# DeltaNet attention and a cosine router: a 32-column inverse, a block-diagonal state and a computed order of steps

## The chip, the cores and the metric

The kernel runs on one core of one Trainium2 chip. A core has five engines, each with its own in-order queue of instructions: TensorE (PE in the profile, PEld for its weight loads), VectorE (DVE), ScalarE (ACT), GpSimd (POOL) and SyncE (SP), which here issues DMAs. [...] Matrix products land in PSUM, eight banks of 2 KB in each of 128 partitions, and VectorE or ScalarE must move them to SBUF, the working memory. The metric is the device time of one execution in microseconds (us). Beside it stands the span, the time from the first to the last instruction in one profiled execution.

## The reference

```python
def _attn_ref(q, k, v, beta):                    # (4, 8, 768, 48) each, beta (4, 8, 768)
    k_n = k / (np.linalg.norm(k, axis=-1, keepdims=True) + 1e-06)
    for t in range(S):
        y[:, :, t] = np.einsum('bhd,bhde->bhe', q[:, :, t], state)
        v_old = np.einsum('bhde,bhd->bhe', state, kt)
        state = state + bt[:, :, :, None] * np.einsum('bhd,bhe->bhde', kt, vt - v_old)
    ...
def _moe_ref(x, expert_emb, tau, w1, w2):        # x (3072, 384), 8 experts, hidden 1024
    logits = xn @ en.T / tau
    expert_idx = np.argmax(logits, axis=1)
    ...
        h = np.maximum(x[mask] @ w1[e], 0.0)
        out[mask] = gate_w[mask, None] * (h @ w2[e])
```

The first half is a linear attention whose 48x48 state for each batch and head is corrected by every token (the delta rule), so tokens depend on each other in order. The second half sends each of the 3,072 tokens to the one of 8 experts whose embedding has the largest cosine with it, and scales the result by the gate. All is in float32.

## The kernel before

The attention works through 12 chunks of 64 tokens (`C`). Of four batches two make a unit: 24 units in all, unit n being chunk n // 2 and batch pair n % 2. Token t of batch i lies in partition 64 i + t, and 8 heads lie along the free dimension. Within a chunk the recurrence becomes linear algebra: a triangular 64x64 matrix for each head and batch, made of products of keys (`gram`, lines 363 to 379), must be inverted, and its inverse applied to the values less what the old state predicts.

The inverse grows by doubling. `W` holds the inverse of the diagonal blocks of 2, and each pair of steps, `level` (line 412) and `grow` (line 417) for s in 2, 4, 8, 16, doubles the block to 32; the last doubling is done on the values by `solve1`, `solve2` and `solve3`. `level` multiplies the gram matrix with the transposed inverse `T`, and VectorE writes the part below the diagonal that the masks `below[s]` name into a prepared identity, `P`; `grow` multiplies `P` with `W`. Both use `product` (line 403): 16 matmuls of 64x64 by 64, of which successive ones take the four quarters of TensorE's array, from partition half a to half b. As the product moves data from one half to the other, an operand is kept in two layouts, and `flip` (line 381) transposes whole 128x128 pairs of heads on TensorE: one for the gram matrix (`a_flip`), three for the inverse (`t_flip`) in every unit. `apply` (line 448) is the other form: one matmul for each head and batch, 16 in all, that stays within its half, so it takes two quarters of the array. The solves and `outputs` use it.

The state lies as `S_u[u]`, a 48x48 block per head and batch in partitions 0 to 47 or 64 to 111; `of_state` (line 425) multiplies it with transposed keys or queries, 16 matmuls of 48x64 by 48. After the outputs come `x_transposes`, `logits` and the routing steps `route1` to `route6`, every second chunk for its four units, and `put_on_lists`, which writes token numbers to per-expert lists in DRAM by indirect DMAs on POOL.

PSUM is shared out as two single banks (`bank`, line 87) and three double ones (`pair`, line 90).

The order of all instructions within their queues is written out by hand: `PLAN` gives each step of a unit a time, units follow each other every `PERIOD` = 20 of those times, and steps are issued in the order of n * PERIOD + time. A step issues its matmuls and its evictions together, so neighbouring dependent steps of a unit stand about 3 times apart and those of three to five units are interleaved between them. `first_weights` loads the first expert's weights on SP in 14 pieces from unit 5 on.

When all lists are written, the expert stage gathers tokens in tiles of 128 by expert and runs both expert layers (`work_through`, line 785): 28 tiles were worked on in the profiled run.

## Time and profile before

| | us |
|---|---|
| median of three timed runs | 800.41 (799.04 to 801.53) |
| profiled execution, own time | 800.33 |
| its span | 798.6 |
| first gram (L325, pair<-KT) | 14.43 |
| first level (pair<-T,AJ) | 28.39 |
| gram of unit 3, gram of unit 23 | 61.8, 406.4 |
| first expert matmul (L723) | 479.7 |
| TensorE busy from 100 to 380 us | 36 to 38 in each 40 |
| POOL pow (L340), each | 1.65 |
| copy_predicated 128x512 (L415), each | 0.73 |
| ScalarE copy, 128x512 and 128x384 | 0.60, 0.49 |

The attention takes the first 480 us and the expert stage the rest. In the profile a line such as `pair<-W,P` names the tile written and those read; L325 is the helper that issues nearly all matmuls, so the groups must be told apart by their tiles: pair<-T,AJ and pair<-T,G are levels, pair<-W,P grows, bank<-ident,W and bank<-ident,G flips, bank<-R,W the first and third solve, bank<-Z,G the second solve and the outputs, pair<-S,KT the state products, pair<-Z,KK the state update, pair<-KT gram. Each float32 matmul makes two records, so 16 matmuls are 32 records; a transposition makes one. Busy times of matmuls overlap, as they are pipelined: what a step takes is read from the start of one step to the start of the next. "issue" as a releaser means that the engine waited for nothing that the profile shows.

### The profile page before, as it was taken

How to read it: one execution, taken by the hardware profiler on the slowest of the kernel's cores; microseconds unless marked ns; L12 is line 12 of the kernel's file. 1: busy time of each engine (PE TensorE's matmuls, PEld its weight loads, DVE VectorE, ACT ScalarE, POOL GpSimd, SP SyncE). 2: the span in 40 equal slices, each digit the busy share in tenths (PEclk: the TensorE clock that was granted, in tenths of full speed). 3: DMA queues.
4: the chain of work that ended last, by engine and by line, in shares of the span. 5: the costliest groups of instructions: out<-in, count | busy, mean ns of one | idle time of the engine just before them, and what ended most of it. 6: DMA issues, size and time to landing. Idle time of an engine off the chain costs nothing.

```text
span 798.6 us, 32885 instructions
## 1 busy us (share of the span) xinstructions
PE 705.7 (88%) x15002; PEld 603.9 (76%) x15002; DVE 281.7 (35%) x644; ACT 240.6 (30%) x463; POOL 223.9 (28%) x257
## 2 busy tenths in 40 slices
PE   2578899998999998999988729999999999999993
PEld 2567888887888887888877628877888877788872
DVE  5465455554555555555544231011011011011010
ACT  3344454454445444445433201001111010111010
POOL 4542333423444342345121121111111111111110
PEclk9699999999999999999999658999999999999997
DMA  6336422321142131111001029999999999999996
GB/s 114 62 109 159 121 39 49 69 41 34 34 86 53 35 77 34 24 25 46 5 5 45 20 49 375 391 367 336 329 316 334 330 313 335 338 319 332 311 323 236
DMA packets 135342, 132.20 MB, mean 166 GB/s; under 512 B 84154, under 2 KB 119393, under 8 KB 135202
## 3 DMA queue, kind: packets, MB, share of 16 engines
q1 hardware_dynamic: 130450, 118.76, 48.3%
q0 software_dynamic: 4544, 11.27, 3.7%
q8 instruction: 119, 1.95, 1.0%
q14 instruction: 21, 0.17, 0.1%
q10 hardware_dynamic: 208, 0.05, 0.0%
HBM read 118.39 MB, written 12.45 MB: 164 GB/s over the span
## 4 chain that ended last, share of the span: by engine, by line
PE 58%; DMA 17%; issue 12%; DVE 6%; ACT 5%; SPq 0%; POOL 0%; POOLq 0%; ACTq 0%; DVEq 0%
PE pair L325 19%; DMA out_dram<-y,ids 16%; PE bank L325 15%; PE acc L723 8%; PE acc L730 7%; PE bank L385 6%; ACT G L373 2%; PE bank L360 1%; PE bank L501 1%; ACT W L401 1%; DVE P L415 1%; DVE W L376 1%; ACT KT L401 1%; DVE XC L492 1%; PE acc L714 1%
## 5 line engine op out<-in xcount | busy, mean ns | idle before, releaser
L725 ACT ACTIVATE hT<-acc 128x512 f32<-128x512 f32 x56 | 33.5, 598 | 279.9 <-PE acc L723 264.7
L723 PEld LDWEIGHTS acc<-xTm,w 128*128 128x128 f32 x864 | 99.3, 192 | 4.8
L723 PE MATMUL acc<-xTm,w 128*128 128x128 f32 x864 | 99.4, 275 | 0.0
L730 PE MATMUL acc<-w,hT 128*128 128x384 f32 x288 | 95.9, 486 | 0.0
L733 POOL DMA_INDIRECT out_dram<-y,ids x28 | 28.5, 1017 | 228.6 <-DVE y L732 211.5
L415 DVE COPY_PREDICATED P<-below,pair 128x512 f32<-128x512 int32 x96 | 70.1, 732 | 51.7 <-PE pair L325 42.4
L325 PE MATMUL pair<-W,P 64*64 64x64 f32 x3072 | 75.6, 224 | 13.3 <-issue 8.3
L401 ACT ACTIVATE W<-pair 128x512 f32<-128x512 f32 x96 | 57.5, 599 | 92.0 <-PE pair L325 86.6
L340 POOL TENSOR_TENSOR rn<-rn,half 128x8 f32<-128x8 f32 x24 | 39.5, 1646 | 139.9 <-DVE rn L339 105.6
L730 PEld LDWEIGHTS acc<-w,hT 128*128 128x128 f32 x288 | 53.3, 190 | 33.4
L325 PEld LDWEIGHTS pair<-W,P 64*64 64x64 f32 x3072 | 64.5, 136 | 17.5 <-issue 10.7
L715 DVE COPY xTm<-acc 128x384 f32<-128x384 f32 x29 | 16.2, 558 | 151.9 <-PE acc L714 151.9
L325 PE MATMUL bank<-Z,G 64*64 64x48 f32 x1536 | 59.6, 225 | 7.9 <-issue 7.5
L325 PE MATMUL bank<-R,W 64*64 64x48 f32 x1536 | 59.3, 223 | 8.1 <-issue 5.5
L732 DVE TENSOR_SCALAR y<-acc,xg 128x384 f32<-128x384 f32 x28 | 17.3, 618 | 129.0 <-PE acc L730 129.0
L325 PEld LDWEIGHTS bank<-R,W 64*64 64x64 f32 x1536 | 53.9, 140 | 10.6 <-issue 10.0
L325 PEld LDWEIGHTS bank<-Z,G 64*64 64x64 f32 x1536 | 53.6, 140 | 9.7 <-issue 8.4
L723 PEld LDWEIGHTS acc<-xTm,w_first 128*128 128x128 f32 x480 | 57.2, 198 | 3.5 <-DVE xTm L715 1.1
L723 PE MATMUL acc<-xTm,w_first 128*128 128x128 f32 x480 | 57.4, 281 | 0.7 <-DVE xTm L715 0.7
L730 PE MATMUL acc<-w_first,hT 128*128 128x384 f32 x160 | 53.3, 486 | 0.0
L325 PE MATMUL pair<-T,AJ 64*64 64x64 f32 x1536 | 40.5, 228 | 11.1 <-DVE T L393 7.0
L385 PE MATMUL bank<-ident,W 128*128 128x128 f32 x288 | 47.9, 289 | 1.3 <-ACT W L401 1.1
(167 smaller groups left out, 987.4 us busy)
## 6 DMA issues: line engine op xcount, KB each, us to landing
w<-in_moe_w_dram SPq DMA_DIRECT2D x40, 1536.0 KB
w_first<-in_moe_w_dram SPq DMA_DIRECT2D x20, 1536.0 KB
x_dram<-XC SPq DMA_DIRECT2D x24, 200.0 KB
k_in<-in_k_dram SPq DMA_DIRECT2D x48, 96.0 KB
QQ<-in_q_dram SPq DMA_DIRECT2D x48, 96.0 KB
v_in<-in_v_dram SPq DMA_DIRECT2D x48, 96.0 KB
idmap<-none SPq DMA_DIRECT2D x1, 1792.0 KB
w_first<-in_moe_w_dram SPq DMA_DIRECT2D x8, 192.0 KB
```

What stands on the lines that cost most here:

```text
L325: nc.tensor.matmul(out_, lhsT=lhsT, rhs=rhs, start=start, stop=True, skip_group_check=True)
L340: nc.gpsimd.tensor_tensor(out=U["rn"], in0=U["rn"], in1=half[:, 0], op=ALU.pow)
L373: nc.scalar.activation(G[:, a].rearrange("p j jj c -> p jj j c"), p[:, :, :, a], ACT.Copy)
L385: nc.tensor.transpose(p[:, j].rearrange("p r c -> p (r c)"), src[:, j].rearrange("p r c -> p (r c)"), ident)
L401: nc.scalar.activation(out_, in_, ACT.Copy)
L415: nc.vector.copy_predicated(U["P"], below[s].broadcast_to(jc), p)
L715: nc.vector.tensor_copy(t.xT, psX)
L723: nc.tensor.matmul(psH[:, i, :], lhsT=t.w1[:, j, (f + i) * 128:(f + i + 1) * 128], rhs=t.xT[:, j, :], start=(j == 0), stop=(j == KC - 1))
L725: nc.scalar.activation(t.hT[:, f:f + 4, :], psH, ACT.Relu)
L730: nc.tensor.matmul(psO, lhsT=t.hT[:, f, :], rhs=t.w2[:, f, :], start=(f == 0), stop=(f == NF - 1))
L732: nc.vector.tensor_scalar_mul(y, psO, t.x[:, Dm:Dm + 1])
L733: nc.gpsimd.indirect_dma_start(out=out[:, :], out_offset=bass.IndirectOffsetOnAxis(ap=t.ids[:, 0:1], axis=0), in_=y, in_offset=None, bound ...
```

## The change

Four things change together.

The inverse is kept in 32 columns a head (`BL`). Up to block size 32 the inverse is block-diagonal in its 64 rows, so both 32-row blocks fit in the same 32 columns: `W` and `T` are 128 x 8 x 32. `G32` is the gram matrix folded in the same way, by two ScalarE copies scaled with row masks. `level` and `grow` now use `apply`, 16 matmuls of 64x64 by 32, in place of `product`. The transposed inverse comes from VectorE's transpose of 32x32 blocks (`transposed_blocks`), straight from the PSUM bank of `grow` while ScalarE copies the same bank to `W`. `flip`, `a_flip` and `t_flip` are gone. `grow_last` spreads the inverse to 64 columns again (`WL`) with two masked copies.

The state gets a second copy, `S_bd`, which puts the blocks of both heads of a pair on the diagonal of a 128-row factor; POOL writes it after each state update with one multiplication by a mask, 128x768. `of_state` then needs 8 matmuls of 128x64 by 96.

PSUM is shared out as four single banks and two double ones.

The order is computed: steps carry assumed costs by engine, and a list scheduler places, one by one, whichever step or part of a step can start earliest, among up to seven units. Steps are generators, so their evictions are placed apart from their matmuls. In the resulting TensorE queue transpositions and x_transposes of two or three units stand together (18 batches of full-array work where there were 103), and between two dependent steps of a unit there stand mostly one or two steps of other units. The first unit's k and q are loaded twice, once ahead of the schedule and once by it. Some preparations move: `K["first"]`, `K["second"]` are made early, and the state's memset goes from POOL to VectorE.

```diff
     def bank(shape):
-        return ps.tile(shape, F32, name="bank", tag="bank", bufs=2)
+        return ps.tile(shape, F32, name="bank", tag="bank", bufs=4)
     def pair(shape):
-        t = ps.tile([128, 2, 512], F32, name="pair", tag="pair", bufs=3)
+        t = ps.tile([128, 2, 512], F32, name="pair", tag="pair", bufs=2)
...
+    def act_copy(out_, in_, scale=1.0):
+        nc.scalar.activation(out_, in_, ACT.Copy, scale=scale)
     def gram(U):
-        KT, p = U["KT"], pair([NP, 2, C])
+        KT = U["KT"]
+        U["psG"] = p = pair([NP, 2, C])
         for j in range(NP):
             for jj in range(2):
                 pr = slice(jj * C, jj * C + D)
                 for i in range(2):
                     mm(p[HALF[i], jj, j], KT[pr, j, 0, HALF[i]], KT[pr, j, :, HALF[i]])
-        G = wk.tile([128, 2, NP, 2, C], F32, name="G", tag="G", bufs=5)
+        yield
+        U["G32"] = wk.tile(hc, F32, name="G32", tag="G32", bufs=3)
+        for b, name in enumerate(("first", "second")):
+            cols = slice(b * BL, (b + 1) * BL)
+            act_copy(by_head(U["G32"])[:, :, :, cols].rearrange("p j jj c -> p jj j c"), p[:, :, :, 0, cols], K[name])
+        yield
+        U["W"] = W2[U["n"] % 2]
+        for b in range(2):
+            cols = slice(b * BL, (b + 1) * BL)
+            nc.vector.copy_predicated(by_head(U["W"]).rearrange("p j jj c -> p jj j c"),
+                                      up2[:, :, cols].unsqueeze(1).broadcast_to([128, 2, NP, BL]), p[:, :, :, 0, cols])
+        yield
+        transposed_blocks(U, U["W"])
+    def gram2(U):
+        p = U["psG"]
+        U["G"] = G = wk.tile([128, 2, NP, 2, C], F32, name="G", tag="G", bufs=5)
         for a in range(2):
-            nc.scalar.activation(G[:, a].rearrange("p j jj c -> p jj j c"), p[:, :, :, a], ACT.Copy)
-        U["A"], U["M"] = {0: G[:, 0]}, G[:, 1]
-        U["W"] = W2[U["n"] % 2]
-        nc.vector.copy_predicated(U["W"].rearrange("p j jj c -> p jj j c"), up2.broadcast_to([128, 2, NP, C]),
-                                  p[:, :, :, 0])
-        M = U["M"].rearrange("p j jj c -> p (j jj) c")
+            act_copy(G[:, a].rearrange("p j jj c -> p jj j c"), p[:, :, :, a])
+            yield
+        M = U["M"] = G[:, 1].rearrange("p j jj c -> p (j jj) c")
         nc.gpsimd.tensor_tensor(M, M, upper.broadcast_to(hc), op=ALU.mult)
-    def flip(src):
-        p = bank(jc)
-        for j in range(NP):
-            nc.tensor.transpose(p[:, j].rearrange("p r c -> p (r c)"), src[:, j].rearrange("p r c -> p (r c)"), ident)
+    def transposed_blocks(U, src):
+        U["T"] = wk.tile([128, H, BL], F32, name="T", tag=f"T{U['n'] % 3}", bufs=1)
+        nc.vector.transpose(U["T"].rearrange("p h c -> p (h c)"), src.rearrange("p h c -> p (h c)"))
+    def apply(lhsT, rhs):
+        p = bank([128, H, rhs.shape[2]])
+        for h in range(H):
+            for i in range(2):
+                mm(p[HALF[i], h], lhsT[HALF[i], h], rhs[HALF[i], h])
         return p
-    def a_flip(U):
-        p = flip(U["A"][0])
-        U["A"][1] = work("AJ", 3)
-        nc.scalar.activation(U["A"][1], p, ACT.Copy)
-        U["T"] = T2[U["n"] % 2]
-        nc.vector.copy_predicated(U["T"], below[1].broadcast_to(jc), p)
-    def t_flip(U, eng):
-        p = flip(U["W"])
-        U["T"] = work("T", 3)
-        eng(U["T"], p)
-    def act_copy(out_, in_):
-        nc.scalar.activation(out_, in_, ACT.Copy)
-    def product(lhsT, rhs):
-        p = pair([NP, C])
-        for j in range(NP):
-            for a in range(2):
-                for b in range(2):
-                    mm(p[HALF[b], a, j], lhsT[HALF[a], j, b], rhs[HALF[a], j, b])
-        return p.rearrange("p a j c -> p j a c")
-    def level(U, s, by):
-        p = product(U["A"][by], U["T"])
+    def level(U, s):
+        p = apply(U["G32"], U["T"])
+        yield
         U["P"] = PP[s][U["n"] % 2]
-        nc.vector.copy_predicated(U["P"], below[s].broadcast_to(jc), p)
+        nc.vector.copy_predicated(U["P"].rearrange("p h (b c) -> p h b c", b=2),
+                                  below[s].rearrange("p o (b c) -> p o b c", b=2).broadcast_to([128, H, 2, BL]),
+                                  p.unsqueeze(2).broadcast_to([128, H, 2, BL]))
     def grow(U):
-        p = product(U["P"], U["W"])
-        U["W"] = work("W", 5)
+        p = apply(U["P"], U["W"])
+        yield
+        U["W"] = wk.tile([128, H, BL], F32, name="W", tag=f"W{U['n'] % 3}", bufs=1)
         act_copy(U["W"], p)
+        yield
+        transposed_blocks(U, p)
+    def grow_last(U):
+        p = apply(U["P"], U["W"])
+        yield
+        U["W"] = wk.tile(hc, F32, name="WL", tag="WL", bufs=3)
+        for b, name in enumerate(("first", "second")):
+            act_copy(U["W"][:, :, b * BL:(b + 1) * BL], p, K[name])
     def by_head(t):
         return t.rearrange("p (j jj) d -> p j jj d", jj=2)
     def of_state(U, a):
-        p = pair([NP, D])
+        p = bank([128, H, D])
         for j in range(NP):
-            for jj in range(2):
-                pr = slice(jj * C, jj * C + D)
-                for i in range(2):
-                    mm(p[HALF[i], jj, j], U["KT"][pr, j, a, HALF[i]], S_u[U["u"]][pr, j, i])
-        return p.rearrange("p jj j d -> p j jj d")
+            for i in range(2):
+                mm(p[HALF[i], 2 * j:2 * j + 2], U["KT"][:, j, a, HALF[i]], S_bd[U["u"]][:, j, i])
+        return p
     def k_state(U):
         V = U["R"]
-        U["R"] = narrow("R")
-        if U["c"] == 0:
+        if U["c"] > 0:
+            p = of_state(U, 0)
+            yield
+        U["R"] = narrow("R", 3)
+        if U["c"] > 0:
+            nc.vector.tensor_tensor(U["R"], p, V, op=ALU.subtract)
+        else:
             nc.vector.tensor_scalar_mul(U["R"], V, -1.0)
-        else:
-            nc.vector.tensor_tensor(by_head(U["R"]), of_state(U, 0), by_head(V), op=ALU.subtract)
     def q_state(U):
         if U["c"] > 0:
+            p = of_state(U, 1)
+            yield
             U["Yq"] = narrow("Yq", 3)
-            act_copy(by_head(U["Yq"]), of_state(U, 1))
-    def apply(lhsT, rhs):
-        p = bank([128, H, D])
-        for h in range(H):
-            for i in range(2):
-                mm(p[HALF[i], h], lhsT[HALF[i], h // 2, h % 2], rhs[HALF[i], h])
-        return p
+            act_copy(U["Yq"], p)
...
+        yield
         S_ = S_u[U["u"]]
         nc.vector.tensor_tensor(S_, p.rearrange("p i j d -> p j i d"), S_, op=ALU.add)
+        yield
+        nc.gpsimd.tensor_tensor(S_bd[U["u"]].rearrange("p j i jj d -> p (j i) jj d"),
+                                S_.rearrange("p j i d -> p (j i) d").unsqueeze(2).broadcast_to([128, H, 2, D]),
+                                K["own"].broadcast_to([128, H, 2, D]), op=ALU.mult)
...
-    PERIOD = 20
-    PLAN = [
-        (-60, load_kq), (-46, prep1), (-42, prep2), (-36, prep3), (-16, load_v), (9.5, scale_v),
-        (-13, lambda U: transposes(U, 0)), (-12.9, lambda U: transposes(U, 1)), (5, gram), (9, a_flip),
-        (13, lambda U: level(U, 2, 1)), (16, grow), (19, lambda U: t_flip(U, nc.vector.tensor_copy)),
-        (23, lambda U: level(U, 4, 0)), (26, grow), (29, lambda U: t_flip(U, nc.vector.tensor_copy)),
-        (35, lambda U: level(U, 8, 1)), (38, grow), (42, lambda U: t_flip(U, act_copy)),
-        (48, lambda U: level(U, 16, 0)), (51, grow),
-        (40, q_state), (41, k_state), (54, solve1), (57, solve2), (64, solve3), (70, state), (72, outputs),
-        (79, x_transposes), (82, logits), (84, last_of_group(route1)), (87, last_of_group(route2)),
-        (91, last_of_group(route3)), (94, last_of_group(route4)), (98, last_of_group(route5)),
-        (103, last_of_group(route6)),
-        (99, put_on_lists(0)), (103.5, put_on_lists(1)), (107, put_on_lists(2)), (111, put_on_lists(3)),
...
+    STEPS = [
+        ("load", lambda U: (load_kq(U), load_v(U)) and None, (), [("SP", 50)]),
+        ("prep1", prep1, ("load",), [("POOL", 9)]),
+        ("prep2", prep2, ("prep1",), [("DVE", 5), ("POOL", 15)]),
+        ("prep3", prep3, ("prep2",), [("DVE", 6), ("POOL", 8)]),
+        ("scale_v", scale_v, ("prep3",), [("POOL", 8)]),
+        ("transposes", transposes, ("prep3",), [("FULL", 16), ("ACT", 6, 0), ("ACT", 6, 0)]),
+        ("gram", gram, ("transposes",), [("PE", 9), ("ACT", 8, 0), ("DVE", 8, 0), ("DVE", 3)]),
+        ("gram2", gram2, ("gram",), [("ACT", 6), ("ACT", 6), ("POOL", 12)]),
     ]
-    events = [
-        (-41, beta_by_token), (-35, more_masks), (-34, lambda: roots(slice(1, NC))), (-12, lambda: fill(PP[2], 1.0)),
-        (6, lambda: fill((W2[1], T2[1]), -1.0)), (7, all_masks), (14, lambda: fill(PP[4], 1.0)),
-        (24, lambda: fill(PP[8], 1.0)), (36, lambda: fill(PP[16], 1.0)),
-        (17, late_constants1), (31, late_constants2), (51, late_constants3),
-        (44, embeddings1), (56, embeddings2), (66, embeddings3),
...
+    before = "gram"
+    for lv in LEVELS:
+        STEPS.append((f"level{lv}", lambda U, lv=lv: level(U, lv), (before,), [("PE", 9), ("DVE", 8)]))
+        before = f"grow{lv}"
+        if lv < LEVELS[-1]:
+            STEPS.append((before, grow, (f"level{lv}",), [("PE", 9), ("ACT", 4, 0), ("DVE", 3, 0)]))
+        else:
+            STEPS.append((before, grow_last, (f"level{lv}",), [("PE", 9), ("ACT", 8)]))
+    STEPS += [
+        ("k_state", k_state, ("transposes", "scale_v"), [("PE", 7), ("DVE", 6)]),
+        ("q_state", q_state, ("k_state",), [("PE", 7), ("ACT", 5)]),
+        ("solve1", solve1, (before, "k_state"), [("PE", 9), ("ACT", 5)]),
+        ("solve2", solve2, ("solve1", "gram2"), [("PE", 9), ("DVE", 6)]),
+        ("solve3", solve3, ("solve2",), [("PE", 9), ("ACT", 5)]),
+        ("state", state, ("solve3", "q_state"), [("PE", 8), ("DVE", 6), ("POOL", 15)]),
+        ("outputs", outputs, ("solve3", "q_state"), [("PE", 9), ("DVE", 6), ("ACT", 6)]),
+        ("x_transposes", x_transposes, ("outputs",), [("FULL", 6), ("ACT", 5)]),
+        ("logits", logits, ("x_transposes",), [("PE", 4), ("DVE", 2)]),
     ]
-    events += [(PERIOD * (5 + i), lambda i=i: first_weights(i)) for i in range(NF + 2 * KC)]
-    steps = [(U["n"] * PERIOD + at, i, U["n"]) for U in UNITS for i, (at, _) in enumerate(PLAN) if i or U["n"]]
-    steps += [(at, -1 - i, 0) for i, (at, _) in enumerate(events)]
-    for _, i, n in sorted(steps):
-        if i < 0:
-            events[-1 - i][1]()
-        else:
-            PLAN[i][1](UNITS[n])
...
+            for n in sorted(waiting)[:7]:
+                for step in waiting[n]:
+                    name, _, needs, cost = step
+                    needs = [(n, x) for x in needs] + [(n - k, x) for y, k, x in EARLIER if y == name and n >= k]
+                    takes = TAKES[name] if cost and cost[0][0] in ("PE", "FULL") else []
+                    for i, (kind, _) in enumerate(takes):
+                        at = len(taken[kind]) + i - bufs[kind]
+                        if 0 <= at < len(taken[kind]):
+                            needs.append(taken[kind][at])
+                    if any(x not in done for x in needs):
+                        continue
+                    start = max([done[x] for x in needs] + [0])
+                    if cost:
+                        first = cost[0][0]
+                        start = max(start, free.get("PE" if first == "FULL" else first, 0))
+                        if first in ("PE", "FULL") and first != mode:
+                            start += 3
+                    if best is None or start < best[0]:
+                        best = start, n, step, takes
...
+    for n, name, f in order():
+        if (n, name) in begun:
+            next(begun[n, name], None)
+            continue
+        for event in EVENTS.get((n, name), ()):
+            event()
+        begun[n, name] = f(UNITS[n])
+        if begun[n, name]:
+            next(begun[n, name], None)
```

## The prediction

> **What bounds the kernel now.** I read the page first, then the waits and the forms of the steady stretch (100 to 380 us), then TensorE's timeline.
>
> ```profile
> PE 705.7 (88%) x15002; PEld 603.9 (76%) x15002; DVE 281.7 (35%) x644; ACT 240.6 (30%) x463; POOL 223.9 (28%) x257
> ...
> PEclk9699999999999999999999658999999999999997
> ...
> q8 instruction: 119, 1.95, 1.0%
> ```
>
> TensorE leads in both stages. From 479.7 us on it is the expert stage, which the diff leaves alone; before that it is the attention, which is all that can move. The clock is low only at 20 to 40 us and at 440 to 480 us. The waits:
>
> ```profile
> POOL KK L349 <- DVE rn L347: 31.6, 11, 3.5
> DVE W L376 <- ACT G L373: 28.7, 17, 2.6
> ...
> PEld pair L325 <- issue: 20.6, 73, 1.1
> ...
> PEld bank L325 <- issue: 12.6, 32, 1.1
> ...
> PEld bank L385 <- ACT KT L401: 3.0, 12, 0.3
> ```
>
> The weight loads wait for other engines hardly at all, but for "issue" 33 us in 280. The timeline tells what that is:
>
> ```profile
> 260.61 0.37 PE L325 MATMUL bank<-Z,G 64*64 64x48 f32 x6 [0.39 <-issue]
> ...
> 264.24 0.39 PE L325 MATMUL pair<-W,P 64*64 64x64 f32 x10 [0.97 <-issue]
> 264.41 1.02 PE L325 MATMUL bank<-Z,G 64*64 64x48 f32 x29
> ...
> 265.33 0.69 PE L325 MATMUL pair<-W,P 64*64 64x64 f32 x29
> 265.96 0.66 PE L385 MATMUL bank<-ident,W 128*128 128x128 f32 x4
> 266.45 0.49 PE L501 MATMUL bank<-ident,XC 128*128 128x128 f32 x3
> ...
> 267.97 0.45 PE L325 MATMUL pair<-S,KT 48*64 48x48 f32 x17 [0.19 <-issue]
> 268.94 0.52 PE L325 MATMUL bank<-enT,xT 128*64 128x8 f32 x12
> 269.39 0.69 PE L325 MATMUL pair<-T,G 64*64 64x64 f32 x32
> ```
>
> The gaps come every 128 pairs of weight load and matmul, at 260.61, 264.24 and 267.97: 3.6 to 3.8 us a block, though the work in a block took as little as 2.4 us. Queue q8 moved 1.95 MB for 30,004 TensorE instructions, 65 bytes each; 119 packets make a block 16 KB. TensorE waits for its own instructions. I take 2.2 us a unit for it (36 us in 280, 17.2 us a unit).
>
> [...] 32 records of Z,G (48 wide, two quarters of the array at a time) take 0.92 us, 58 ns a couple, and 12 records of enT,xT, only 8 wide, still 0.35 us, again 58. [...] Here a change between 64-column and 128-column work costs some 0.24 us there and back beyond its steps. [...]
>
> **The change part by part.** Starts of successive steps give TensorE's prices: a product over four quarters 0.50 us (Z,KK at 258.23, the next at 258.73), an `apply` over two quarters 0.93, a transposition 0.109, gram 0.90, a state product 0.47, x_transposes 0.33, logits 0.35, route3 1.43.
> - Removed: 16 flips a unit, 1.74 us, and most mode changes: full-array batches fall from 103 to 18, but 44 state products now hold all 128 rows between 64-row steps. Leaving a 128-row step costs 0.075 us more than a normal step in the trace; entering I take at 0.1. In all 14 us instead of 24.5.
> - Levels and grows become `apply`, two quarters and 32 wide. By the 8-wide row width saves nothing under the 58 ns floor: 0.93 us each, 192 of them, +81 us. Were it paid by width, 16 couples at some 32 ns would make 0.51.
> - k_state and q_state: 16 records, 96 wide, K=128. Gram's four quarters at 128 wide need 110 ns; 85 ns a couple gives 0.68 us, against 0.47: +9 us. If the two column halves could not overlap it would be 1.3, but gram's share their rows and do.
> - The sum of TensorE work: 24 x (0.87+0.90+7.44+2.79+0.93+0.33+0.35) + 22 x (1.36+0.48) + 7 x 1.43 = 377 us, against 328 before.
> - Instruction waits: 503 pairs a unit instead of 554, and a block of pure `apply` work takes 3.7 us by itself, just what a block needs to arrive. I keep 0.15 us a unit of the 2.2: 4 us in all, 50 saved. State products (15 ns a pair) can still outrun the supply.
> - Evictions. Level to grow: 0.25 us from the last matmul to VectorE, copy_predicated 0.73, 0.05 back: 1.03. Grow to level: ScalarE copies 128x256 (0.38, from 0.49 at 384 and 0.60 at 512), and only then may VectorE transpose out of the same bank. Its transpose is not in the trace: [...] I take 0.43: 1.2 us. Between grow and its level TensorE has only one other step (0.93) in about 32 of 72 cases.
> - POOL gains the block-diagonal copy, 128x768; from 0.83 (384) and 1.28 (512) it is 1.7 to 2.2, and I take 1.9. It stands between state and k_state two units on; the queue has 2.8 us of other work there in 12 of 22 cases, as much as the path needs if POOL is free. Behind a pow (1.65) it is late, and the PE queue with it.
>
> To see what these do together I followed every queue by hand through one stretch, gram of unit 16 to gram of unit 18: 37.9 us of TensorE work. It stood still 0.68, 0.30, 0.07, 0.27 and 0.25 us at levels waiting for T, 0.65 and 0.2 at k_state waiting for POOL, 0.3 at transpositions waiting for banks: 2.7 us, 7%.
>
> Head. Unit 0's k and q are now loaded twice; its squares wait for the second copy, 4.4 us later on SP, half of it under the beta path, so gram 0 starts at about 16.5 us instead of 14.4. But it no longer waits for a flip and three masks: the first level starts near 24 us, not 28.4. Work to gram of unit 3 is 33.8 us; half clock 5, stalls 4, modes 2: 69 us, where before it is 61.8 (before has less done by then).
> Middle, to gram of unit 23: 300.5 us of work, 7% stalls 21, modes 12.5, instructions 3.5: 337.5 us; before 344.6.
> Tail, to the end of the last route3: 39.3 us, 7% is 3, half clock 4, the last unit's bare solve chain 4.5, modes 1: 52 us; before 59.5.
> Sum 458.5 against 465.9: 7.4 us earlier. The 14 us of list transfers and gathers after it and the expert stage stay. Span 798.6 becomes 791.2; the profiled execution took 800.3, 1.7 more, and the median shown is 800.4, so 793, and as the ends round downward, 792.
>
> The other edits hide: preparation order, masks and moved memsets are on VectorE and POOL, each under 60% busy in the stretch. Without that cover the masks cost 2 us. Loads on SP are issued earlier and in another order; weights of the first expert still come hundreds of us before use.
>
> **Rivals.**
> 1. *The transpose becomes the bound (slower).* At 0.72 us it adds 0.29 to each grow-to-level wait; five of six in my stretch were already exposed, so over 24 units 19 us, and in-order queues add as much on other chains: 805 to 825. It decides from about 0.60 us. For it: one step of cover. Against: VectorE is only 57% busy. POOL's copy at 2.2 and behind pow does the same for 5 to 8 us.
> 2. *Instruction waits stay* in proportion to pairs: 2.0 us a unit, 44 us more: 836. Against: blocks whose work lasts 3.6 us show almost no gap.
> 3. *The stalls vanish* (3% or less): 773 to 778. Against: the bank order forces ScalarE before VectorE.
> 4. *Width pays*: `apply` at 0.51 saves up to 80 us of work, chains then bind, some 750. The 8-wide row speaks against it.
> 5. *The gains and losses cancel*: stalls at 9%, 798 to 803.
>
> **How the numbers follow.** The mechanism above (780 to 798): 0.40. Stalls small, or width paid: 0.12, faster. Cancelling: 0.13, of it 0.10 within 0.3%, which is about what a measurement of this kernel can tell from no change (2.4 us), and 0.03 slower. Rival 1: 0.31, rival 2: 0.04, both slower. Faster 0.52, same 0.10, slower 0.38. The likeliest case's own range is 780 to 798; over all, 772 to 822.
>
> **What would show it.** Right: level and grow groups of 32 records in 0.93 us; "issue" before weight loads under 0.5 us a unit; the first expert matmul at 470 to 474 us; TensorE's waits on VectorE T and POOL S_bd some 7% of the stretch; units 16.9 us apart. Wrong: a transpose over 0.6 us, state products near 1.3, gaps still every 128 pairs, or units more than 17.5 us apart, which is slower than before.

## The result and the profile after

The changed kernel took 888.9 us (865.01 to 914.18, four runs), the kernel before beside it 799.72 us (798.27 to 801.53): a ratio of 1.087, interval 1.077 to 1.098. Ratios here and below leave out runs of a kernel that took over 1.5% longer than its fastest; by the medians this one is 1.11. The runs of the changed kernel lie far apart, and the longer ones have the lower mean granted clock: 0.895, 0.884, 0.878 and 0.837 for 865, 874, 904 and 914 us. How the times follow the clock is loose, though: 904 and 874 us differ by more than 0.878 and 0.884 account for. The profiled run is the fastest: 865.01 us, span 863.3. The prediction was 792, range 772 to 822.

The page of the changed kernel: busy times, TensorE's granted clock in 40 slices, and the instruction queue.

```profile
PE 795.6 (92%) x13914; PEld 713.1 (83%) x13914; DVE 285.1 (33%) x696; ACT 220.6 (26%) x485; POOL 254.4 (29%) x277
...
PEclk9975999985855899899998985799999999999998
...
q8 instruction: 111, 1.82, 0.8%
```

TensorE has 7% fewer instructions than before and is busy 90 us longer. The second line is the answer to it: where before there were two low places, at the head and ahead of the expert stage, there are now 5s and 8s in the midst of the attention. The waits from 100 to 380 us, as line, releaser, us in total, times, longest:

```profile
DVE T L412 <- ACT W L376: 46.4, 35, 3.5
...
PEld bank L334 <- issue: 7.9, 21, 1.3
...
PEld bank L334 <- DVE T L412: 2.8, 9, 0.7
```

The waits for instructions fell from 33 us to 8. VectorE's transpose does stand behind ScalarE's copy (each of the 72 out of a bank begins 0.03 to 0.60 us after the copy's end), 46 us in sum, but only 2.8 us of it reach TensorE's weight loads. So TensorE waits for little, and yet is late. The same stretch cut into 40 us (start and end, length, then busy us of TensorE, its weight loads, VectorE, ScalarE and POOL with counts, granted clock, DMA share, GB/s):

```profile
60.00:100.00 40.00, 40.00 (x857) 38.45 (x855) 16.15 (x40) 13.45 (x31) 10.04 (x12) 0.70 0.31 89
100.00:140.00 40.00, 38.79 (x1282) 37.54 (x1278) 22.73 (x46) 15.18 (x37) 13.05 (x12) 1.00 0.35 87
140.00:180.00 40.00, 39.79 (x1202) 37.98 (x1199) 19.23 (x43) 16.69 (x40) 10.60 (x10) 1.00 0.17 34
180.00:220.00 40.00, 38.47 (x660) 36.67 (x658) 13.78 (x42) 13.70 (x29) 18.89 (x21) 0.62 0.19 43
220.00:260.00 40.00, 38.87 (x866) 38.14 (x862) 18.22 (x37) 10.72 (x26) 10.81 (x10) 0.64 0.14 28
260.00:300.00 40.00, 39.22 (x737) 37.26 (x735) 13.77 (x37) 13.06 (x30) 12.87 (x15) 0.64 0.20 45
```

The busy column says 96 to 100% in every row. The count and the clock say what happened: 1,282 and 1,202 matmul records at clock 1.00, 660 to 866 at 0.62 to 0.64. A busy TensorE at half clock looks like a busy TensorE. Single steps on its timeline (start, length, records) show the two speeds:

```profile
49.01 1.07 PE L334 MATMUL bank<-W,P 64*64 64x32 f32 x32
49.91 1.10 PE L334 MATMUL bank<-T,G 64*64 64x32 f32 x32
...
209.67 1.92 PE L334 MATMUL bank<-W,P 64*64 64x32 f32 x32
211.40 1.82 PE L334 MATMUL bank<-R,WL 64*64 64x48 f32 x30
```

From start to start a grow takes 0.90 us at full clock and 1.73 at half. The groups of two operations that the trace of before did not have:

```profile
L412 DVE STREAM_TRANSPOSE T<-bank 128x256 f32<-128x256 f32 x72 | 32.4, 449 | 78.2 <-ACT W L376 78.0
L504 POOL TENSOR_TENSOR S_bd<-S,own 128x768 f32<-128x768 f32 x22 | 32.3, 1466 | 158.5 <-DVE S L502 153.9
```

The transpose takes 0.449 us, POOL's block-diagonal copy 1.466.

The trace also records each stretch of half clock, in multiples of 3.41 us (the last is cut off by the end). Up to the start of the attention's last matmul I add these up; half of them is an estimate of the time lost (too high where TensorE would have waited for another engine in that time anyway), and what remains is called net:

| kernel (profiled execution) | last attention matmul | recorded at half clock before it | lost | net |
|---|---|---|---|---|
| before | 465.6 | 39.5 | 19.8 | 445.8 |
| changed | 530.4 | 156.2 | 78.1 | 452.3 |

The attention ends 64.8 us later, as the span does (863.3 against 798.6). By this estimate 58 of it is clock and 6.5 all the rest.

The table leaves something out. The records of the clock begin only with its first stretch at full speed: at 46.5 us in the changed kernel, at 23.3 in the kernel before. The page prints a 9 for the time ahead of that, but the steps there have the pace of half clock. In the changed kernel:

```profile
33.56 3.60 PE L334 MATMUL bank<-W,P 64*64 64x32 f32 x64
36.97 3.60 PE L334 MATMUL bank<-T,G 64*64 64x32 f32 x64
```

Two grows of 32 records take 3.41 us from start to start, 1.70 each. From the first gram on this adds 30 us of half clock in the changed kernel and 9 in the kernel before, by the same estimate up to 15 and 4 us lost, so the clock can account for all of the 64.8 us. The sums of half clock below are the recorded ones, unless the head is named. Net is rough: the same kernel's trace from another chip (further down) comes to 443.3 instead of 452.3, so differences of net under some 10 us say nothing.

### The profile page after: what moved, and what is told of

Its sections match the earlier page's. It is cut to its first block, busy times and chain, and to the rows that moved or that the text cites. A ratio compares the mean times of both kernels' runs of the same rounds, so it can differ in the third digit from the quotient of the medians.

```text
span 863.3 us, 30826 instructions
## 1 busy us (share of the span) xinstructions
PE 795.6 (92%) x13914; PEld 713.1 (83%) x13914; DVE 285.1 (33%) x696; ACT 220.6 (26%) x485; POOL 254.4 (29%) x277
## 4 chain that ended last, share of the span: by engine, by line
PE 74%; DMA 11%; issue 6%; DVE 5%; ACT 1%; POOL 1%; SPq 1%; POOLq 0%; ACTq 0%; DVEq 0%
PE bank L334 44%; PE acc L884 11%; PE acc L891 10%; DMA out_dram<-y,ids 10%; PE pair L334 4%; PE bank L369 3%; PE bank L531 1%; DVE T L412 1%; ACT W L376 1%; PE acc L875 1%; DVE W L396 1%; DVE P L426 0%; SPq L122 0%; POOL rn L347 0%; DMA xg<-x_dram,ids 0%
## 5 line engine op out<-in xcount | busy, mean ns | idle before, releaser
L334 PE MATMUL bank<-T,G 64*64 64x32 f32 x3072 | 118.6, 233 | 9.1 <-DVE T L412 7.5
L334 PEld LDWEIGHTS bank<-T,G 64*64 64x64 f32 x3072 | 111.4, 152 | 14.3 <-DVE T L412 6.5
L334 PE MATMUL bank<-W,P 64*64 64x32 f32 x3072 | 117.0, 233 | 1.8 <-DVE P L426 1.8
L334 PEld LDWEIGHTS bank<-W,P 64*64 64x64 f32 x3072 | 111.2, 152 | 4.8 <-ACT Yq L376 1.2
L884 PE MATMUL acc<-xTm,w 128*128 128x128 f32 x864 | 99.4, 275 | 0.0
L426 DVE COPY_PREDICATED P<-below,bank 128x512 f32<-128x512 int32 x96 | 69.5, 729 | 67.3 <-PE bank L334 67.1
L504 POOL TENSOR_TENSOR S_bd<-S,own 128x768 f32<-128x768 f32 x22 | 32.3, 1466 | 158.5 <-DVE S L502 153.9
L334 PE MATMUL bank<-R,WL 64*64 64x48 f32 x1536 | 66.9, 246 | 2.3 <-issue 2.3
L334 PEld LDWEIGHTS bank<-Z,G 64*64 64x64 f32 x1536 | 61.8, 160 | 7.1 <-issue 5.3
L334 PEld LDWEIGHTS bank<-R,WL 64*64 64x64 f32 x1536 | 61.8, 162 | 3.6 <-issue 2.8
L412 DVE STREAM_TRANSPOSE T<-bank 128x256 f32<-128x256 f32 x72 | 32.4, 449 | 78.2 <-ACT W L376 78.0
L884 PE MATMUL acc<-xTm,w_first 128*128 128x128 f32 x480 | 56.9, 280 | 0.7 <-DVE xTm L876 0.7
L347 POOL TENSOR_TENSOR rn<-rn,half 128x8 f32<-128x8 f32 x24 | 39.5, 1644 | 57.5 <-DVE rn L345 56.6
```

Source lines behind the costliest of these rows:

```text
L334: nc.tensor.matmul(out_, lhsT=lhsT, rhs=rhs, start=start, stop=True, skip_group_check=True)
L347: nc.gpsimd.tensor_tensor(out=U["rn"], in0=U["rn"], in1=half[:, 0], op=ALU.pow)
L412: nc.vector.transpose(U["T"].rearrange("p h c -> p (h c)"), src.rearrange("p h c -> p (h c)"))
L426: nc.vector.copy_predicated(U["P"].rearrange("p h (b c) -> p h b c", b=2), below[s].rearrange("p o (b c) -> p o b c", b=2).broadcast_to([1 ...
L504: nc.gpsimd.tensor_tensor(S_bd[U["u"]].rearrange("p j i jj d -> p (j i) jj d"), S_.rearrange("p j i d -> p (j i) d").unsqueeze(2).broadcas ...
L884: nc.tensor.matmul(psH[:, i, :], lhsT=t.w1[:, j, (f + i) * 128:(f + i + 1) * 128], rhs=t.xT[:, j, :], start=(j == 0), stop=(j == KC - 1))
```

## Experiments

**What a matmul gives the clock.** The first theory, A, is that the clock is granted by how much streams through the array, not by how long TensorE is busy. Take the share of the array's cells that a group uses, times the columns it streams, per time, and the expert stage's 128x128 matmuls (128 columns every 0.112 us from start to start) as 1. A `product` of before, 32 records of 64 columns on a quarter in 0.50 us, stands at 0.9; a level or grow of the changed kernel, 32 records of 32 columns in 0.93 us, at 0.24. In the trace of before, matmuls 8 and 48 columns wide (enT,xT and Z,G) both step 58 ns a couple (two pairs of weight load and matmul), so by the author's estimate width should be free: streaming every operand twice gives 0.48 at no cost. Four kernels ran on one chip, where the kernel before took 789.79 us (783.05 to 796.54).

*Levels and grows made wide.* Every right-hand operand of `level`, `grow` and `grow_last` is streamed twice, and the second copy of the result is not read:

```diff
+    def apply_wide(lhsT, rhs):
+        p = bank([128, 2, H, BL])
+        ...
+                mm(p[HALF[i], :, h], lhsT[HALF[i], h], rhs[HALF[i], h].unsqueeze(1).broadcast_to([C, 2, BL]))
+        return p[:, 0]
-        p = apply(U["G32"], U["T"])
+        p = apply_wide(U["G32"], U["T"])
```

> The changed kernel with one edit: in level and grow the 32 moving columns are streamed twice (64 columns, the second copy of the result is not read), so the results are the same. Theory A (the clock of TensorE is halved when too few columns stream through the array in a window, and narrow two-quarter steps stream too few): a step still takes 0.93 us, [...] but the mean granted clock rises from 0.895 to 0.95 or more, and the time falls to 790 to 800 us. Theory B (the clock falls because TensorE stands still at waits in between): the waits are the same, so clock 0.86 to 0.90 and 860 to 900 us. Theory C (the width is paid for): 192 steps grow to more than 0.93 us and it is slower than 889 us.

801.85 us (801.03 to 803.53), ratio 1.019 (1.014 to 1.025), clock 0.964. Useless work on TensorE alone brought the ratio from 1.087 (on the first chip) to 1.019. The windows of this kernel, as above:

```profile
180.00:220.00 40.00, 36.26 (x1099) 34.44 (x1099) 25.92 (x58) 17.33 (x41) 24.09 (x24) 1.00 0.32 66
220.00:260.00 40.00, 37.54 (x1042) 35.16 (x1038) 21.89 (x52) 18.21 (x42) 22.71 (x24) 1.00 0.31 64
260.00:300.00 40.00, 38.93 (x1138) 37.01 (x1134) 20.65 (x53) 16.35 (x38) 13.35 (x15) 1.00 0.17 33
```

TensorE is a little less busy than in the narrow kernel and issues 1.2 to 1.7 times the matmuls, at clock 1.00. At half clock before the attention's end there are 27.8 us instead of 156.2, and the first full clock comes at 27.5 us instead of 46.5. At full clock a level or grow that another two-quarter step follows takes 0.93 to 0.98 us from start to start, where the narrow one takes 0.92 to 0.96: width is nearly free.

*Levels alone wide*, four of the eight steps in each unit's chain:

> As the run before, but only level streams its columns twice, grow does not. Theory A: half of the dose, mean clock between 0.90 and 0.95 and 805 to 850 us. Theory B: as the changed kernel, 860 to 900 us.

803.81 us (801.49 to 808.85), ratio 1.024 (1.016 to 1.031), clock 0.961. Half the dose is nearly as good as the whole: the effect is not in proportion to it. The expected clock of 0.90 to 0.95 was too low.

*The kernel before with 16 columns.* The converse: less streaming in a kernel that has its clock. `product` streams 16 of 64 columns, and its two evictions move 16.

```diff
-                    mm(p[HALF[b], a, j], lhsT[HALF[a], j, b], rhs[HALF[a], j, b])
+                    mm(p[HALF[b], a, j, 0:NCOL], lhsT[HALF[a], j, b], rhs[HALF[a], j, b, 0:NCOL])
```

A product then stands at 0.22, as a level of the changed kernel does.

> The kernel before, but each product (levels and grows) streams 16 of its 64 columns, and the evictions behind it move those 16 alone; the other 48 columns of every inverse are left out, so the inverse is not the one wanted. It has the same matmuls, weight loads and order as before, and less work for VectorE and ScalarE. Theory A: clock falls in the attention from 0.957 in the mean to 0.93 or less, and the attention takes 15 to 60 us longer although work was taken away. Theory B: the queue has as few waits as before, so the clock stays at 0.95 to 0.96 and the attention is as long as before or some us shorter.

881.06 us (868.99 to 937.47), in the profiled run clock 0.860 and a span of 867.3 us. Two of its windows:

```profile
100.00:140.00 40.00, 36.88 (x1102) 34.13 (x1102) 14.33 (x34) 14.14 (x33) 10.66 (x12) 0.79 0.44 112
180.00:220.00 40.00, 40.00 (x885) 37.75 (x883) 11.67 (x27) 10.68 (x24) 10.08 (x12) 0.50 0.15 31
```

A kernel from which work was taken away (but for the filling of five tiles in its head) became slower by some 90 us; its attention ends at 535 us, 70 after that of before, more than the 15 to 60 expected. At half clock stand 217 us by the records, which begin at 99.4 us only; ahead of that its products step 53 ns a couple, as they do in the half-clock stretches, against 29 at full clock. Theory A holds in both directions, and this kernel has nothing of the change in it: no 32-column inverse, no VectorE transposes, no computed order. The numbers that it multiplies are other ones, too, so that they play a part is not excluded here; the wide kernel multiplies the same numbers as the changed one.

*Wide, and two small edits.* Unit 0's k and q are loaded once, and VectorE transposes a grow's bank before ScalarE copies it; the order of steps is computed again with that in its costs.

```diff
-        ("load", lambda U: (load_kq(U), load_v(U)) and None,
+        ("load", lambda U: (U["n"] and load_kq(U), load_v(U)) and None,
-        act_copy(U["W"], p)
-        yield
         transposed_blocks(U, p)
+        yield
+        act_copy(U["W"], p)
-     [("PE", 9), ("ACT", 4, 0), ("DVE", 3, 0)]
+     [("PE", 9), ("DVE", 4, 0), ("ACT", 4, 1)]
```

> The wide kernel (levels and grows stream 64 columns), and two more edits: unit 0's k and q are loaded once, and VectorE transposes out of a grow's bank before ScalarE copies from it. Theory A with the working of the prediction: clock 0.95 or more, gram 0 near 14.5 us, the waits of levels on T shorter by 0.38 us each, so 780 to 792 us. Theory B: 850 to 895 us, at a clock under 0.91.

779.07 us (775.08 to 782.04), ratio 0.988 (0.984 to 0.991): faster than both kernels. Clock 0.975.

**Waits or width?** The edits of the last kernel also shorten TensorE's waits, so the clock could have been lost through waits that wide products hide. A second set ran on another chip, beside the kernel before at 789.69 us (787.1 to 795.35).

*The two edits without the width:*

> The changed kernel with the two small edits of the fastest kernel so far and without its wide products: unit 0's k and q are loaded once, and VectorE transposes a grow's bank before ScalarE copies it; levels and grows stay 32 columns wide. Theory A (the clock is lost because 32-wide products stream little through the array): the clock is still lost, mean 0.86 to 0.92, 840 to 880 us, though TensorE waits less for T than in the changed kernel. Theory B (the clock is lost through TensorE's waits for T, which both edits shorten and wide products happen to hide): clock 0.96 or more, 775 to 790 us, as with wide products.

811.5 us, between both expectations, and spread from 798.79 to 834.8 with mean clocks from 0.974 to 0.900; no ratio is given over such a spread. Windows of the profiled run, 798.79 us:

```profile
60.00:100.00 40.00, 39.17 (x1053) 38.28 (x1051) 16.54 (x34) 12.35 (x30) 8.91 (x9) 0.79 0.18 44
100.00:140.00 40.00, 38.20 (x786) 37.04 (x784) 16.87 (x42) 12.33 (x29) 12.81 (x14) 0.66 0.28 74
140.00:180.00 40.00, 39.96 (x1250) 38.70 (x1246) 20.66 (x45) 16.52 (x39) 11.90 (x10) 1.00 0.17 32
```

The clock is still halved for 27 us at a time, twice, and 58 us in all, against 156 in the changed kernel and 13 with the same edits and wide products (the head ahead of the records, from the first gram on, adds 24, 30 and 11). Theory A alone had expected 840 to 880 and is too simple. Theory B, waits alone, had expected 775 to 790 and is refuted: wide products with the same edits take 779. The reading that fits, an interpretation, is that width and waits count together: narrow groups leave so little streaming that a window with some waits in it falls short, and fewer waits mean fewer such windows.

*Wide, transpose first, but unit 0 loaded twice:*

> Wide levels and grows, VectorE's transpose before ScalarE's copy, but unit 0's k and q still loaded twice; beside the fastest kernel it gives the price of the second load, beside the wide kernel that of the order of the two evictions. Theory A: the first gram stands at 14.6 us with one load and 16.4 with two, so this is 2 us slower than one load (about 0.3%) and the order of evictions is worth the other 20 of 22.8 us: ratio to before 0.988 to 0.994. Theory B: the second load sits ahead of later loads and keeps costing; then this stands nearer to the wide kernel, ratio 1.00 to 1.02, and the order of evictions is worth less than half.

782.69 us (778.79 to 787.04), ratio 0.990 (0.987 to 0.993). The first gram stands at 16.4 us with two loads and at 14.6 with one. The second load is worth about what was expected, 0.002 of the ratio, with intervals that overlap; transpose order and new order of steps together take the ratio from 1.019 to 0.990.

*Filling the wait before the expert stage:*

```diff
+    for i in range(12):
+        nc.tensor.matmul(acc([128, 512]), lhsT=ident, rhs=w1_first[:, 0, 0:512], start=True, stop=True)
     transposed(work[0])
```

> The fastest kernel so far (wide, one load, transpose first) with 12 matmuls of the whole array, 128x512 each, whose results nobody reads, put between the attention's last matmul and the first expert tile, where TensorE otherwise waits 12.5 us for the lists and gathers. There the clock was halved from 441.5 to 462.0 us, 4.8 us of it under expert work. Theory A (the clock follows how much the array streams): no half clock in that wait or after it, the first expert matmul at the same time within 1 us, 2 to 4 us saved, ratio to before lower by 0.003 to 0.005 than without them. Rival: the matmuls only delay the first expert tile, 0 to 8 us lost.

776.96 us (774.65 to 777.09), ratio 0.983 (0.979 to 0.987), against 0.988 (0.984 to 0.991) without the filling on another chip: the expected difference of 0.005, but the intervals overlap. The windows from 444 us on show what it did, first of the kernel without the filling:

```profile
444.00:458.00 14.00, 1.88 (x8) 1.46 (x8) 5.57 (x33) 0.22 (x1) 4.03 (x5) 0.50 0.25 62
458.00:462.00 4.00, 3.29 (x16) 3.25 (x16) 0.56 (x1) 0.00 (x0) 0.00 (x0) 0.50 0.95 328
```

and, of the kernel with the filling:

```profile
444.00:458.00 14.00, 13.72 (x27) 5.96 (x27) 5.47 (x33) 0.21 (x1) 4.03 (x5) 0.78 0.30 73
458.00:462.00 4.00, 3.30 (x29) 3.23 (x29) 0.56 (x1) 0.12 (x1) 0.00 (x0) 1.00 1.01 401
```

The expert stage begins at full clock, 29 matmul records in its first 4 us instead of 16. Its first matmul stands where it stood, at 457.6 us against 457.2. Not expected: the clock stayed at half until 450.2 us, 6 us into the filling. That is the end of the first window of 3.41 us (446.8 to 450.2) that the filling takes up whole.

*The kernel before, on the same chip:*

> The kernel before, unchanged, for its trace on the chip of the other three. Theory: here too its clock is halved only in the head, for a window or two in the middle and around the wait before the expert stage, 20 to 32 us of time lost before the first expert matmul; a time below 795 us goes with fewer halved windows, and TensorE's work by group is the same.

786.17 us in this single run. The kernel before took 785 to 791 us on the later chips, 8 to 15 less than on the first. At half clock before the attention's end stand 25.9 us by the records and 22.8 in the head ahead of them (they begin at 37.3 us); in the kernel with the filling it is 10.4 and 9.0. That kernel ends its attention 8.8 us earlier (443.5 against 452.3), its span is 9.1 us shorter, and it has no half clock in the first 5.9 us of expert work. Half of the difference in half clock, some 15 us, is more than that. So the clock can account for the whole gain; that the attention of the changed design is any shorter without it does not show.

**What starts a drop.** In the head of the changed kernel a drop at 53.35 us, 6.8 us after the first full clock, lasts 30.7 us. Its timeline just before, of VectorE, POOL and TensorE (start, length, engine, line, operation):

```profile
51.32 2.80 DVE L268 CAST iota_e<-iota_ei 128x8 f32<-128x8 int32 x1 [0.22 <-POOL iota_ei L266]
...
52.84 1.25 POOL L408 TENSOR_TENSOR G<-G,upper 128x512 f32<-128x512 f32 x1
...
54.50 0.42 DVE L412 STREAM_TRANSPOSE T<-W 128x256 f32<-128x256 f32 x1
...
55.08 0.32 PE L334 MATMUL bank<-T,G 64*64 64x32 f32 x2 [4.07 <-DVE T L412]
```

and the same conversion in the kernel before, by its minimum, median and maximum in ns:

```profile
L259 DVE CAST iota_e<-iota_ei x1: 149/149/149, 42.5 to 42.5; 128x8 f32<-128x8 int32 x1
```

Eight numbers a partition take 0.149 us before and 2.80 us after: the conversion ends at 54.12 us, 0.03 after the last of three POOL instructions that follow each other without a gap. In the kernel with wide products and the two edits it took 2.02 us and ended 0.03 us after the last of two POOL instructions. Why the conversion takes as long as they do was not tested. T stands behind the conversion and TensorE stands 4.07 us. Does this wait start the drop? The values exist already in another table:

```diff
-        iota_ei = ac.tile([128, E], I32, name="iota_ei")
-        nc.gpsimd.iota(iota_ei, pattern=[[1, E]], base=0, channel_multiplier=0)
-        iota_e = ac.tile([128, E], F32, name="iota_e")
-        nc.vector.tensor_copy(iota_e, iota_ei)
+        iota_e = col_f[:, 0:E]
```

The third set, on a chip where the kernel before took 784.96 us (779.53 to 789.58), has the changed kernel unedited, with this edit, and the fastest kernel with it.

> The changed kernel, unedited, beside the next two on their chip. Theory: the time is that of the net work, about 452 us to the attention's end, plus half of all time at half clock before it; 850 to 910 us, ratio to before 1.07 to 1.13, and runs that are longer show a lower mean clock.

863.11 us (834.95 to 889.63), 10% over the kernel before there by the medians, so the slowness is not that of one chip. Its longest run has the lowest clock (0.859), its shortest the highest (0.952). But in the profiled run net is 443.3 us, not the expected 452 (194.2 us at half clock before the last attention matmul at 540.2 us): half of the time at half clock is too much as a measure of the loss.

> The changed kernel, all products narrow, but without the conversion of a small index table (128x8, integer to float) on VectorE and its making on POOL; the values are taken from a table that exists already. In the changed kernel that conversion took 2.80 us at 51 us while POOL worked, T and P stood behind it, TensorE stood 4.07 us, and the clock was halved from 53.35 us for 30.72 us. Theory A (a wait starts the drop, and narrow work cannot lift the clock again): no half clock from 50 to 85 us, gram of unit 3 some 18 to 22 us earlier (4 of the wait, 15 of the clock), the later drops remain, so 835 to 880 us, 10 to 25 us less than the unedited kernel. Theory B (narrow work alone, without any wait, halves the clock): half clock begins within 15 us of the same place and lasts, less than 8 us saved.

844.84 us (837.0 to 860.49), ratio 1.066 (1.059 to 1.073). Gram of unit 3 moved from 86.45 to 81.32 us, 5.1 us, and the clock was halved all the same, from 51.37 us for 23.9 us. In the head these are the numbers of theory B, though the median, 18 us under that of the run before, lies where theory A had it. The words of theory B don't fit either, as the window of 3.41 us ahead of the drop shows:

```profile
47.96:51.37 3.41, 2.45 (x86) 2.34 (x78) 2.34 (x9) 2.92 (x9) 2.14 (x4) 1.00 0.59 114
```

TensorE was busy for 2.45 us of it: after the long wait was gone a shorter one came, 1.50 us for the same T. So both theories fall as they were put: it doesn't take 4 us of waiting to start a drop, and it was not narrow work without any wait. The windows ahead of two drops in the midst of the changed kernel say the same:

```profile
183.06:186.47 3.41, 2.87 (x99) 2.66 (x95) 1.20 (x3) 0.74 (x2) 1.00 (x1) 1.00 0.01 2
227.43:230.84 3.41, 2.40 (x80) 2.25 (x75) 3.01 (x8) 1.17 (x3) 1.46 (x2) 1.00 0.48 89
```

TensorE stands still for 0.5 and 1.0 us in them. In the kernel before, two of many windows that kept the clock:

```profile
190.55:193.96 3.41, 2.39 (x129) 2.27 (x125) 1.37 (x3) 1.20 (x3) 0.00 (x0) 1.00 0.03 6
262.23:265.64 3.41, 2.44 (x130) 2.30 (x129) 0.90 (x3) 1.35 (x4) 0.00 (x0) 1.00 0.02 5
```

It stands still as long there, for instructions, and the next window is at full clock. Where its groups stream 0.9 of the rate while they run, a window with 1 us of waiting still comes to 0.45 or 0.46 by the measure above; the two windows of the changed kernel come to 0.22 and 0.23. The rest of the difference between the medians of this kernel and the unedited one is not settled, as it lies within the spread of the latter; its fastest run, 834.95 us, is no slower than any here.

> The same edit in the fastest kernel so far (wide, one load, transpose first, matmuls in the wait before the expert stage). There TensorE stood 4.66 us at 44 to 48 us and the clock was halved from 47.4 us for 6.83 us. Theory A: 4.7 us of the wait and 3.4 of the clock go, less what of it is slack: 769 to 774 us, ratio to before 0.974 to 0.980. Theory B: another wait takes its place there (the list of masks or a load), 775 to 777 us, ratio 0.982.

771.25 us (770.13 to 775.68), the lowest time of all, but the kernel before was fast on this chip too: ratio 0.983 (0.978 to 0.987), what it was without the edit. Theory B: the 4.66 us wait is gone, and TensorE is only 7.15 us busy in the 10 us from 50 on.

**The order of the two evictions.** Of the step from 1.019 to 0.990, what is the swap of ScalarE's copy and VectorE's transpose, and what the order of steps computed anew? One kernel has the swap alone; the order in the queues of all engines but ScalarE is unchanged. It ran on another chip, where the kernel before took 791.29 us (786.56 to 793.73).

> The wide kernel with one edit: VectorE transposes a grow's bank before ScalarE copies it. The order of steps is not computed anew: TensorE's, VectorE's, POOL's and SyncE's queues are those of the wide kernel instruction for instruction, and ScalarE's differs by one neighbouring pair. With the order computed anew for this edit the ratio to before was 0.990, without the edit 1.019. Theory A (the prediction's price: ScalarE must read before VectorE, 0.38 us and a hand-over in each of 72 chains, most of them exposed): most of the 0.029 comes from the edit itself, ratio 0.990 to 1.003. Theory B: the new order of steps brings it; ratio 1.008 to 1.019.

798.11 us (796.45 to 799.74), ratio 1.008 (1.004 to 1.012). The swap is worth 0.011, the new order of steps 0.018, with some 0.006 of uncertainty on each, and the ratios compared are from three chips. In the waits from 100 to 380 us TensorE's weight loads stood 5.2 us for T in 18 places without the swap and 1.5 us in 4 with it. The result lies at the edge of theory B: the larger part is the order of steps.

## Why the prediction was wrong

**The step that failed** is the clock in the sum of Head, Middle and Tail: "half clock 5" in the head, "half clock 4" in the tail and none in the middle, 9 us in all, where the profiled run lost about 78 by the records and up to 15 more in the head. The prediction gave the changed kernel half clock in the head and the tail alone, as it read it in the kernel before ("only at 20 to 40 us and at 440 to 480"; in fact it was low before 23 us, too), and priced operations in time alone. Even the gain that it forecast came from the clock: the kernel before lost some 20 us of its 465.9 to half clock by the records, the sum of 458.5 allowed 9, so that without the clock the sum stood at 449.5 us against 446. It even had the fact in hand: levels and grows took 0.93 us for half the columns and half the quarters, so that the array had about a quarter of the work per time. No rival and no entry under "Wrong" named the clock. TensorE need not stand idle for it: at 186.47 us the clock was lost after a window of 3.41 us in which TensorE was busy for 84% with narrow work, and at half clock windows busy for 99 to 100% did not bring it back.

**The rest of the sum held in the main.** The wide kernel has the same order of steps and nearly the clock of before, and so tests it. Gram of unit 3 started at 70.6 us, where the prediction had 69; from there to gram of unit 23 it took 340.8 us (70.58 to 411.41), where it had 337.5, with 3.4 lost to the clock and none allowed for; from there to the last matmul of the attention 56.9, where it had 52, with 7.1 lost and 4 allowed for. Together that is 468.3 us against 458.5. The middle comes out at 337.4 us without the clock, in part by luck: its weight loads stood still for 23.3 us, where the prediction had 24.5 (stalls 21, instructions 3.5), but only 9.8 of it for T and S_bd (3% of the stretch, not 7), and 6.1 for instructions. Two small sums of the prediction are off: mode changes are 14 us in one place and 2, 12.5 and 1 in another, and 192 steps of 0.93 instead of 0.50 us are 83 us more, not 81.

- *Levels and grows at 0.93 us whatever the width*: 0.92 to 0.96 at full clock where another two-quarter step follows, 0.93 to 0.98 for twice the columns. Rival 4, that width pays, is refuted; width pays in the opposite sense.
- *State products 0.68*: 0.81 from start to start at full clock, with the changes of mode that the prediction priced apart (0.075 and 0.1); within the step a couple takes 82 to 83 ns, where it had 85. *Transpose 0.43*, the author's estimate, which no trace of before showed: 0.449, so rival 1 (over 0.60) did not come. *POOL's copy 1.9*: 1.47, below the range of 1.7 to 2.2.
- *Instruction waits, 0.15 us a unit kept*: 7.9 us of weight loads' waits from 100 to 380 us, and 2.5 in the wide kernel, which has full clock throughout that stretch. Rival 2 is refuted; the 2.5 are 0.15 a unit, though over the longer stretch above it is 0.3.
- *Units 16.9 apart*: in the changed kernel's stretch at full clock, units 4 and 7 begin at 101.31 and 152.49 us, 17.06 apart each; in the wide kernel it is 17.04 over 20 units.
- *Rival 3, the stalls vanish, 773 to 778, "the bank order forces ScalarE before VectorE"*: it took a new order of evictions and of steps, and wide products, to see it: 779 us. The bank order was worth 0.011 of the ratio, the order of steps more.
- *The first expert matmul at 470 to 474*: 544.8 us, and 482.9 in the wide kernel.

That the wide kernel is 2% over the kernel before on its chip, where the prediction had 1% under, has two parts of about 1.3% each. Its span, 801.8 us, is 10.6 over the predicted 791.2, some 5 of it clock. And the kernel before was 10 us faster on that chip than on the first. Why is open; in its trace from the chip of the second set its weight loads stood 30.0 us for "issue" from 100 to 380 us, against 35.7 on the first, which may be part of it.

## What to carry to other kernels

Before trading wide matmuls for narrow ones, work out how much of the array the new groups fill per time, and look at what the old ones filled (0.24 and 0.9 of the expert stage's rate here): levels and grows took 0.92 to 0.96 us at 32 columns and 0.93 to 0.98 at 64, so narrower operands saved nothing there, and they cost the clock (0.895 against 0.964). When TensorE is nearly 100% busy and late, compare counts of matmuls in equal stretches and the granted clock before looking for waits; where the clock's records have not begun, time a known step. If the clock is what is missing, streaming an operand twice is a quick test and, where a step takes as long at twice the width, a remedy: here it brought the ratio from 1.087 to 1.019.

## What was not expected of the hardware

- In these runs the clock followed streaming and not busy time alone. In the changed kernel the window of 3.41 us ahead of each of the eight drops up to the attention's end stood at 0.05 to 0.28 of the expert stage's rate, though other windows of 0.22 to 0.28 passed without a drop; in the kernel before, most stood at 0.39 to 0.75. Windows busy for 97% and more at about 0.22 kept the clock in the changed kernel, and in the kernel before with 16 columns four of seven drops follow fully busy windows of 0.21 to 0.32. No sharp threshold shows, and what exactly is counted, cells or columns, stays open.
- Half clock lasted where narrow work went on: at half clock most fully busy windows of the changed kernel stood at 0.13 to 0.30 of the rate, and stretches of it lasted up to 51 us in the changed kernel and 72 us in the kernel before with 16 columns, but 3 to 7 us in the midst of the wide kernels. It is so from the start: the first full clock came at 46.5 us in the changed kernel and at 99.4 in the kernel before with 16 columns, at 23.5 to 27.9 in the kernels with wide products.
- The changed kernel's times spread over some 6% on one chip, those of the kernels with wide levels and grows over 0.3 to 1.1%. Whether a window falls short seems to turn on how the steps lie in the windows; that was not tested.
- A conversion of 128x8 on VectorE took 2.80 us while three POOL instructions ran back to back, 2.02 us with two, and 0.149 us with none.
